# Attention's numerators in 64 array rows and 256 columns a call, with the units loaded by quarters of the partitions

## The chip, the cores and the metric

One core of a Trainium2 chip runs the kernel. The metric is the device time of one launch in microseconds (us). The engines are named as in the profile: PE (TensorE matmuls), PEld (TensorE weight loads), DVE (VectorE), ACT (ScalarE), POOL (GpSimd) and SP (SyncE, which here only issues DMAs). Each engine works through its own list of instructions in order.

## The reference

A block of a transformer: 2048 tokens, width 1024, 32 heads of 32, a hidden layer of 3584. Attention is linear, with a learned feature map of two softmaxes:

```python
def _A_ref(x, wqkv, w_phi, wo):
    q, k, v = ...                        # x @ wqkv, by heads
    pq = einsum("bhsd,hdf->bhsf", q, w_phi)
    pk = einsum("bhsd,hdf->bhsf", k, w_phi)
    phi_q = concatenate([softmax(pq), softmax(-pq)], axis=-1)
    phi_k = concatenate([softmax(pk), softmax(-pk)], axis=-1)
    kv = einsum("bhsf,bhsd->bhfd", phi_k, v)
    z  = einsum("bhsf->bhf", phi_k)
    num = einsum("bhqf,bhfd->bhqd", phi_q, kv)
    den = einsum("bhqf,bhf->bhq", phi_q, z)[..., None] + 1e-6
    o = num / den
    return o (heads side by side) @ wo
h  = x + _A_ref(layernorm(x), wqkv, w_phi, wo)
h2 = h + relu(layernorm(h) @ w1) @ w2
```

The map gives 64 features for a head: 32 of the positive sign and 32 of the negative. In the text, "sign" is this half of the features.

## The kernel before, in words

The program is one long list of items of eight steps. A step is three matmuls of 128x512 (`mm3`, L182 to L184), because each fp32 operand is split into a high and a low part. Beside the steps stands a table, `at[n, k]`: the work that is to be written into the program before step k of item n. `when(8 * n + k, f)` and `do(n, k, f)` fill it. So the order of everything beside the large matmuls, on every engine, follows from numbers in this table; at run time an engine waits when the head of its own list is not ready.

The items run in this order: keys and values of the first 1024 tokens (`kv`, 32 items), queries of them (`q`, 16), keys and values of the second 1024 tokens, their queries, the output projection (`wo`), then the two layers of the feed-forward part (`up`, `down`). The `wo` items begin at item `wo_first`.

**Feature map of q.** `q_first` (DVE) takes maximum and minimum and writes both signs' arguments into a tile; `q_second` (ACT) exponentiates and stores the 512 KB tile to DRAM (`ed`); `q_third` (DVE) sums over the 32 features and inverts (`smq`, the softmaxes' inverse sums, kept in SBUF).

**Sums over k.** `kv_third` (PE, L464) accumulates kv for four heads at a time; at the end `kv_turn` transposes it with TensorE to `kvL` and `z_sum` adds the keys' features over the partitions (`zb`).

**Attention units.** The rest is cut into 32 units u, each of four token tiles (one of four groups b) and four of the 32 heads. For each unit run, in this order:

- `at_load` (SP, L543): one DMA of 512 KB from `ed`; `at_sums` (POOL, L575): two products with `zb`, 128x512 each; `at_reduce` (DVE, L581): their sums over 32 features;
- `at_den` (POOL, L591 and L595): times the inverse sums, and the two signs added, which lie side by side in the free dimension; `at_inverse` (DVE, L598);
- `at_scale` (POOL, L608 and L613): inverse sum times inverse denominator, and the 128x1024 product of the unit with it; `at_turn` (DVE, L619): transposition in blocks of 32x32.

After an odd unit, `at_num` (PE, L633) multiplies the pair by `kvL`: 64 calls in tiles of 32 rows and 32 columns of the array, 128 tokens a call, which the profile shows as 128 records. Each PSUM bank has a row group's results; four banks are used, two of the pool `tp` (two banks in all, which transposes use too) and two of `ac`. ACT copies the four banks to `oT` (L640), and `at_low` (DVE, L651) takes the rest of the split, four times.

I number the pairs k = 0 to 15; units 2k and 2k+1 are E and O below. Units 0 to 5 have sums and denominators done early. From u = 12 the steps of an even unit are, relative to its start, 7 for the load, 14 sums, 18 reduce, 20 denominator, 22 inverse, 24 scale, 28 turn; `at_num` comes at step 38 and `at_low` at step 40. So a pair's `at_low` is written while the next pair's denominators are under way. The first units of `wo` overlap with the last groups of the attention.

**The second layer norm's first half** also runs in the `wo` stage: `ln_pair` has nine stages for each i = 0..3 (load, statistics, power, normalize, three turns of four TensorE transposes each, one with sums, one more with sums), and `ln_store` stores the results. `NEAR` gives their steps.

The weights' splitting (L125 on ACT, L129 on POOL or DVE) goes on all the time.

Of the kernel before, what the change touches and what calls it, by code (L numbers as in the profile page):

```python
# [140 lines left out]
def kernel(  # L141
# [55 lines left out]
    ed = [dram.tile([P, 8, 4, 256], F32, name=f"ed{b}") for b in range(4)]  # L197
# [257 lines left out]
    def kv_third(key):  # L455
# [12 lines left out]
        for g in range(2):  # L468
            ps = kv_ps[s][g][:, 0:64]
            if hf == 0:  # L470
                v.tensor_copy(kvacc[s][:, g, :], ps)
            else:
                kd_of[s, g] = kd = kp.tile([P, 2, 4, 32], F32, name="kd", bufs=2)
                for sd in range(2):
                    part = slice(32 * sd, 32 * (sd + 1))
                    v.tensor_add(kd[:, sd, :, :], ps[:, None, part].to_broadcast([P, 4, 32]),
                                 kvacc[s][:, g, None, part].to_broadcast([P, 4, 32]))

    def kv_turn(s):
        pt = tp_bank()  # L480
        for g in range(2):
            for sd in range(2):
                pe.transpose(pt[:, (2 * sd + g) * P:(2 * sd + g + 1) * P],
                             kd_of[s, g][:, sd].rearrange("p c f -> p (c f)"), ident)
        v.tensor_copy(kvL[:, 4 * s:4 * s + 4, :], pt.rearrange("p (g n) -> p g n", g=4))

    def z_sum(s):


        pz = tp_bank()  # L490
        pe.matmul(pz, ones, zacc[s], start=True, stop=True)
        act.activation(zb[:, s, :].rearrange("p (r c x) -> p c r x", r=2, c=4),
                       pz.rearrange("p (c r x) -> p c r x", r=2, c=4), AF.Identity, bias=eps)
# [17 lines left out]
    def q_first(s, t, ps):  # L511

        pq = ps.rearrange("p (h f) -> p h f", f=32)
        m = pqp.tile([P, 2, 16], F32, name="qmx", bufs=2)
        v.tensor_reduce(out=m[:, 0, :], in_=pq, op=ALU.max, axis=AX.X)
        v.tensor_reduce(out=m[:, 1, :], in_=pq, op=ALU.min, axis=AX.X)
        e = pqp.tile([P, 16, 2, 32], F32, name="qe", bufs=2)
        v.tensor_sub(e[:, :, 0, :], pq, m[:, 0, :, None].to_broadcast([P, 16, 32]))
        v.tensor_sub(e[:, :, 1, :], m[:, 1, :, None].to_broadcast([P, 16, 32]), pq)
        e_of[s, t] = e  # L520

    def q_second(s, t):
        act.activation(e_of[s, t], e_of[s, t], AF.Exp)
        b, i = place_of[t]
        act.dma_start(ed[b][:, 4 * s:4 * s + 4, i, :], e_of[s, t].rearrange("p (a c) s f -> p a (c s f)", a=4))

    def q_third(s, t):
        b, i = place_of[t]
        sm = smq[:, 4 * b + i, 32 * s:32 * (s + 1)]
        v.tensor_reduce(out=sm, in_=e_of.pop((s, t)).rearrange("p h s f -> p (h s) f"), op=ALU.add, axis=AX.X)  # L530
        v.reciprocal(sm, sm)

# [6 lines left out]
    def at_load(u):  # L539

        e = lnp.tile([P, D], F32, name="xin") if u in (4, 5, 10, 11) else ap_.tile([P, D], F32, name="qe", bufs=4)
        e_q[u] = e = e.rearrange("p (h s f) -> p h s f", s=2, f=DH)
        sp.dma_start(e.rearrange("p (i c) s f -> p i (c s f)", i=4), ed[u // 8][:, u % 8])  # L543

# [4 lines left out]
    def early_load(u):  # L549
        e_q[u] = e = xlp.tile([P, D], F32, name="xl").rearrange("p (h s f) -> p h s f", s=2, f=DH)  # L550
        sp.dma_start(e.rearrange("p (i c) s f -> p i (c s f)", i=4), ed[u // 8][:, u % 8])

    def early_sums(u):
        b, q, r = UNITS[u]
        e = e_q[u].rearrange("p (i h) s f -> p i (h s f)", i=4)
        pool.tensor_tensor(out=e, in0=e, in1=zb[:, q, None, 256 * r:256 * (r + 1)].to_broadcast([P, 4, 256]),
                           op=ALU.mult)

    def early_reduce(u):
        tz_of[u] = tz = xlp.tile([P, 32], F32, name="xtz", bufs=2)  # L560
        v.tensor_reduce(out=tz, in_=e_q.pop(u).rearrange("p h s f -> p (h s) f"), op=ALU.add, axis=AX.X)

    def early_scale(u):
        den = den_of.pop(u)
        sm = sm_half(u).rearrange("p i (h s) -> p i h s", s=2)
        pool.tensor_tensor(out=sm, in0=sm, op=ALU.mult,
                           in1=den.rearrange("p (i h) -> p i h", i=4)[:, :, :, None].to_broadcast([P, 4, 4, 2]))

    def at_sums(u):

        b, q, r = UNITS[u]
        for j in range(2):
            third = hp is not None and (2 * u + j) % 3 == 2
            ez_of[u, j] = ez = (hp if third else ap_).tile([P, 2, 256], F32, name="ez", bufs=1 if third else 2)
            pool.tensor_tensor(out=ez, in0=e_q[u].rearrange("p (i h) s f -> p i (h s f)", i=4)[:, 2 * j:2 * j + 2, :],  # L575
                               in1=zb[:, q, None, 256 * r:256 * (r + 1)].to_broadcast([P, 2, 256]), op=ALU.mult)

    def at_reduce(u):
        tz_of[u] = tz = ap_.tile([P, 32], F32, name="qtz", bufs=2)
        for j in range(2):  # L580
            v.tensor_reduce(out=tz[:, 16 * j:16 * (j + 1)], in_=ez_of.pop((u, j)).rearrange("p i (h f) -> p (i h) f", f=DH),  # L581
                            op=ALU.add, axis=AX.X)

    def sm_half(u):
        b, q, r = UNITS[u]
        return smq[:, 4 * b:4 * b + 4, 16 * q + 8 * r:16 * q + 8 * r + 8]

    def at_den(u):

        tz = tz_of.pop(u)  # L590
        pool.tensor_tensor(out=tz.rearrange("p (i h) -> p i h", i=4), in0=tz.rearrange("p (i h) -> p i h", i=4),  # L591
                           in1=sm_half(u), op=ALU.mult)
        tz2 = tz.rearrange("p (h s) -> p h s", s=2)
        den_of[u] = den = (ap_ or xlp).tile([P, 16], F32, name="qden", bufs=2)
        pool.tensor_tensor(out=den, in0=tz2[:, :, 0], in1=tz2[:, :, 1], op=ALU.add)  # L595
# [4 lines left out]
    def at_scale(u):  # L600
        if u < EARLY:
            e = e_q.pop(u).rearrange("p (i c) s f -> p i (c s) f", i=4)
            pool.tensor_tensor(out=e, in0=e, in1=sm_half(u)[:, :, :, None].to_broadcast([P, 4, 8, 32]), op=ALU.mult)
# [706 lines left out]
```

## Time and profile before

| | |
|---|---|
| median of 3 runs | 1883.05 us (1880.56, 1883.05, 1883.9) |
| the profiled execution: its time, its span | 1883.67 us, 1881.9 us |
| PE busy | 1871.4 us, 99% |
| DVE, ACT, POOL busy | 1070.6, 739.0, 973.1 us |
| clock granted to TensorE | 0.999 |
| attention's numerators on PE (L633) | from 552.0 us to 759.9 us |

A busy share counts an engine over the whole span, over stages with different limits. The attention's part of the trace, 550 to 760 us, is where the change works, so stage views of that part are read below.

### The profile page before, as it was taken

How to read it: one execution, taken by the hardware profiler on the slowest of the kernel's cores; microseconds unless marked ns; L12 is line 12 of the kernel's file. 1: busy time of each engine (PE TensorE's matmuls, PEld its weight loads, DVE VectorE, ACT ScalarE, POOL GpSimd, SP SyncE). 2: the span in 40 equal slices, each digit the busy share in tenths (PEclk: the TensorE clock that was granted, in tenths of full speed). 3: DMA queues.
4: the chain of work that ended last, by engine and by line, in shares of the span. 5: the costliest groups of instructions: out<-in, count | busy, mean ns of one | idle time of the engine just before them, and what ended most of it. 6: DMA issues, size and time to landing. Idle time of an engine off the chain costs nothing.

```text
span 1881.9 us, 31799 instructions
## 1 busy us (share of the span) xinstructions
PE 1871.4 (99%) x11608; PEld 1535.3 (82%) x11608; DVE 1070.6 (57%) x1695; ACT 739.0 (39%) x1271; POOL 973.1 (52%) x959
## 2 busy tenths in 40 slices
PE   9999999999999999999999999999999999999999
PEld 7877788888787888878888888888888888888887
DVE  7788688677689777555554563444433333343333
ACT  5322245222233122255455554444444444444442
POOL 4887744888946988333233222222344444444443
PEclk9999999999999999999999999999999999999999
DMA  6888788656565666887888985666677677767775
GB/s 225 290 293 289 227 296 258 199 190 200 185 217 177 203 226 221 259 258 217 258 254 263 320 273 176 192 191 215 210 238 215 204 228 238 238 213 219 216 216 178
DMA packets 303277, 432.17 MB, mean 230 GB/s; under 512 B 24208, under 2 KB 165520, under 8 KB 303120
## 3 DMA queue, kind: packets, MB, share of 16 engines
q1 hardware_dynamic: 286224, 413.36, 70.0%
q10 hardware_dynamic: 16896, 16.78, 2.7%
q8 instruction: 91, 1.49, 0.3%
q14 instruction: 66, 0.54, 0.1%
HBM read 292.68 MB, written 137.36 MB: 229 GB/s over the span
## 4 chain that ended last, share of the span: by engine, by line
PE 95%; DMA 2%; POOL 1%; DVE 1%; issue 0%; ACT 0%; SPq 0%; DVEq 0%; ACTq 0%; POOLq 0%
PE mm L182 25%; PE mm L183 24%; PE mm L184 24%; PE ac L183 4%; PE ac L182 4%; PE ac L184 4%; PE tp L183 2%; PE tp L184 2%; PE tp L182 2%; PE tp L245 1%; PE ac L464 1%; PE tp L633 1%; DMA hT<-hs 1%; DMA hs<-xin 1%; PE ac L633 1%; POOL w L129 0%
## 5 line engine op out<-in xcount | busy, mean ns | idle before, releaser
L129 POOL TENSOR_TENSOR w<-raw,w 128x512 fp32r<-128x512 f32 x353 | 469.2, 1331 | 719.8 <-ACT w L125 674.8
L125 ACT ACTIVATE w<-raw 128x512 fp32r<-128x512 f32 x686 | 409.0, 626 | 508.0 <-PE mm L184 235.0
L129 DVE TENSOR_TENSOR w<-raw,w 128x512 fp32r<-128x512 f32 x333 | 271.4, 816 | 519.5 <-ACT w L125 514.1
L182 PE MATMUL mm<-w,xT 128*128 128x512 f32 x768 | 305.3, 398 | 0.0
L183 PE MATMUL mm<-w,xT 128*128 128x512 f32 x768 | 299.8, 390 | 0.6 <-POOL w L400 0.4
L184 PE MATMUL mm<-w,xT 128*128 128x512 f32 x768 | 299.3, 390 | 0.0
L183 PE MATMUL mm<-hT,w 128*128 128x512 f32 x672 | 262.1, 390 | 2.8 <-DVE hT L829 2.8
L182 PE MATMUL mm<-hT,w 128*128 128x512 f32 x672 | 262.2, 390 | 0.0
L184 PE MATMUL mm<-hT,w 128*128 128x512 f32 x672 | 262.0, 390 | 0.0
L362 POOL TENSOR_TENSOR b<-b 128x256 f32<-128x256 f32 x176 | 143.5, 816 | 55.1 <-DMA b<-in_w_dram 36.9
L182 PEld LDWEIGHTS mm<-w,xT 128*128 128x128 f32 x768 | 144.2, 188 | 33.9 <-issue 2.9
L184 PEld LDWEIGHTS mm<-w,xT 128*128 128x128 f32 x768 | 144.2, 188 | 30.7
L183 PEld LDWEIGHTS mm<-w,xT 128*128 128x128 f32 x768 | 144.3, 188 | 29.9 <-POOL w L129 1.0
L182 PE MATMUL mm<-w 128*128 128x512 f32 x392 | 152.5, 389 | 0.0
L183 PE MATMUL mm<-w 128*128 128x512 f32 x392 | 152.5, 389 | 0.0
L184 PE MATMUL mm<-w 128*128 128x512 f32 x392 | 152.5, 389 | 0.0
L183 PEld LDWEIGHTS mm<-hT,w 128*128 128x128 f32 x672 | 126.6, 188 | 29.6 <-DVE hT L829 3.3
L184 PEld LDWEIGHTS mm<-hT,w 128*128 128x128 f32 x672 | 126.6, 188 | 26.4
L182 PEld LDWEIGHTS mm<-hT,w 128*128 128x128 f32 x672 | 126.4, 188 | 26.3
L182 PEld LDWEIGHTS mm<-w 128*128 128x128 f32 x392 | 73.6, 188 | 15.3
L183 PEld LDWEIGHTS mm<-w 128*128 128x128 f32 x392 | 73.6, 188 | 15.3
L184 PEld LDWEIGHTS mm<-w 128*128 128x128 f32 x392 | 73.6, 188 | 15.2
(184 smaller groups left out, 3147.9 us busy)
## 6 DMA issues: line engine op xcount, KB each, us to landing
raw<-t SPq DMA_DIRECT2D x224, 256.0 KB, 3.9
raw<-ad SPq DMA_DIRECT2D x196, 256.0 KB, 3.0
raw<-in_w_dram SPq DMA_DIRECT2D x168, 256.0 KB, 3.1
ad<-c SPq DMA_DIRECT2D x112, 256.0 KB, 3.6
b<-in_w_dram SPq DMA_DIRECT2D x44, 512.0 KB, 6.0
t<-b SPq DMA_DIRECT2D x44, 512.0 KB, 4.8
ad<-s SPq DMA_DIRECT2D x84, 256.0 KB, 3.9
ed<-qe ACTq DMA_DIRECT2D x32, 512.0 KB, 4.4
```

The source lines that it names most:

```text
L125: nc.scalar.activation(w[:, 0, :], raw[1], AF.Copy)
L129: eng.tensor_tensor(out=w[:, 1, :], in0=raw[1], in1=w[:, 0, :].bitcast(F32), op=ALU.subtract)
L182: pe.matmul(ps, a_hi, b_hi, start=first, stop=False, skip_group_check=more)
L183: pe.matmul(ps, a_hi, b_lo, start=False, stop=False, skip_group_check=more)
L184: pe.matmul(ps, a_lo, b_hi, start=False, stop=last, skip_group_check=more)
L245: pe.transpose(pt[:, k, :], xn[:, (4 * j + k) * P:(4 * j + k + 1) * P], ident)
L362: pool.tensor_tensor(out=tsum[*u, *out], in0=tsum[*u, *a], in1=tsum[*u, *b], op=ALU.subtract)
L464: pe.matmul(kv_ps[s][g][32 * i:32 * (i + 1), 0:64], vt[:, 32 * h:32 * (h + 1)], phi[:, 64 * h:64 * (h + 1)], start=first, stop=last)
L633: pe.matmul(banks[g][32 * c:32 * (c + 1), j * P:(j + 1) * P], kvL[rows, 4 * q + 2 * sd + h // 4, 32 * (h % 4):32 * (h % 4 + 1)], phT_of[u ...
```

## The change

Four pieces belong together.

1. **Numerators.** `at_num` has 16 calls: 64 rows (both signs of 32 features) and 256 columns. It fills two banks of `ac`, and none of `tp`. ACT then copies two banks of 512 columns, and `at_low` has two instructions. `kvL` therefore holds both signs along the rows, `kv_turn` does two TensorE transposes for four heads where it had four, and `kd` is made with one addition.

2. **Layout.** For 64 rows both signs of the same tokens must lie in neighbouring blocks of 32 partitions once a unit has been turned. So `q_first` writes the tile sign by sign in groups of four heads, and `by_quarter` reads a unit in four DMAs of 32 partitions each: a quarter has one sign and one pair of token tiles. Each of the 32 units has four loads of 128 KB where it had one of 512 KB. The inverse sums `smq` are needed in the same layout: `sm_store` writes them to DRAM and `sm_load` reads them back in four DMAs (`smx`), once for each of the four groups.

3. **Denominators.** The two signs of a token now lie in different partitions. `at_den` keeps its first product; the new `at_cross` copies four 32x32 blocks on ACT to the other sign's partitions, and the new `at_add` (POOL) adds. The inverse (DVE) and the products have 32 columns, where the inverse had 16. `z_sum` writes `zb` in four ACT instructions of 32 partitions where it had one.

4. **Steps.** The lists of steps get the two new stages, and `NEAR` becomes one list for all i, by which the turns of a pair are written as eight transposes twice. Some fill in the SBUF pools is smaller.

```diff
-    ed = [dram.tile([P, 8, 4, 256], F32, name=f"ed{b}") for b in range(4)]
+    ed = [dram.tile([8, 4, P, 256], F32, name=f"ed{b}") for b in range(4)]
+    smd = [dram.tile([4, P, 64], F32, name=f"smd{b}") for b in range(4)]
...
+    def by_quarter(dst, src):
+        for a in range(4):
+            sp.dma_start(dst[32 * a:32 * (a + 1)],
+                         src[2 * (a // 2):2 * (a // 2) + 2].rearrange("i (n t) (s x) -> s t (i n) x", t=32, s=2)[a % 2])
...
     def at_den(u):
-        tz = tz_of.pop(u)
-        pool.tensor_tensor(out=tz.rearrange("p (i h) -> p i h", i=4), in0=tz.rearrange("p (i h) -> p i h", i=4),
-                           in1=sm_half(u), op=ALU.mult)
-        tz2 = tz.rearrange("p (h s) -> p h s", s=2)
-        den_of[u] = den = (ap_ or xlp).tile([P, 16], F32, name="qden", bufs=2)
-        pool.tensor_tensor(out=den, in0=tz2[:, :, 0], in1=tz2[:, :, 1], op=ALU.add)
+        tz = tz_of[u].rearrange("p (n c) -> p n c", n=8)
+        pool.tensor_tensor(out=tz, in0=tz, in1=sm_half(u), op=ALU.mult)
+    def at_cross(u):
+        den_of[u] = den = (ap_ or xlp).tile([P, 32], F32, name="qden", bufs=2)
+        for a in range(4):
+            act.activation(den[32 * (a ^ 1):32 * (a ^ 1) + 32], tz_of[u][32 * a:32 * (a + 1)], AF.Copy)
+    def at_add(u):
+        pool.tensor_tensor(out=den_of[u], in0=tz_of.pop(u), in1=den_of[u], op=ALU.add)
...
     def at_num(u):
-        acc_of[u] = banks = tp_bank(), tp_bank(), ac_bank(), ac_bank()
-        for sd in range(2):
-            for j in range(2):
-                for g in range(4):
-                    rows = slice(32 * g, 32 * (g + 1))
-                    for c in range(4):
-                        pe.matmul(banks[g][32 * c:32 * (c + 1), j * P:(j + 1) * P], ...)
+        acc_of[u] = banks = ac_bank(), ac_bank()
+        for j in range(2):
+            for g in range(2):
+                rows = slice(64 * g, 64 * (g + 1))
+                for c in range(4):
+                    pe.matmul(banks[g][32 * c:32 * (c + 1), 256 * j:256 * (j + 1)], ...)
...
-        stages = (-8, 6, 10, 13, 16, 19, 25) if u < 12 else (7, 14, 18, 20, 22, 24, 28) if u % 2 == 0 else \
-            (-1, 9, 13, 15, 17, 19, 23)
+        stages = (-8, 6, 10, 13, 15, 17, 18, 20, 26) if u < 12 else (7, 14, 18, 20, 21, 23, 24, 25, 29) if u % 2 == 0 else \
+            (-1, 9, 13, 15, 16, 18, 19, 20, 24)
...
-    NEAR = {1: (0, 9, 12, 17, 29, 30, 31, 32, 34, 37), 2: (4, 14, 17, 21, 25, 26, 27, 28, 30, 36)}
+    NEAR = 0, 9, 12, 17, 24, 24, 27, 27, 30, 36
```

The pair k = 12 (units 24 and 25) shows how the lists of POOL, DVE and ACT change. In these rows a name's number tells one tile from another. First POOL before, from the first denominator to the first product of the next pair: `qtz_8311` and `qden_8324` belong to E, `qtz_8329` and `qden_8413` to O.

```order
L591 TENSOR_TENSOR qtz_8311<-qtz_8311,smq_2995 128x32
L595 TENSOR_TENSOR qden_8324<-qtz_8311 128x16
L591 TENSOR_TENSOR qtz_8329<-qtz_8329,smq_2995 128x32
L595 TENSOR_TENSOR qden_8413<-qtz_8329 128x16
L608 TENSOR_TENSOR qsd_8427<-smq_2995,qden_8324 128x32
L613 TENSOR_TENSOR qe_8226<-qe_8226,qsd_8427 128x1024
L608 TENSOR_TENSOR qsd_8441<-smq_2995,qden_8413 128x32
L613 TENSOR_TENSOR qe_8228<-qe_8228,qsd_8441 128x1024
L575 TENSOR_TENSOR ez_8460<-qe_8415,zb_2993 128x512
```

Both denominators are whole before E is scaled. POOL in the changed kernel, at the same place, where `qden_7946` is E's and `qden_8000` O's:

```order
L602 TENSOR_TENSOR qtz_7930<-qtz_7930,smx_3000 128x32
L611 TENSOR_TENSOR qden_7946<-qtz_7930,qden_7946 128x32
L602 TENSOR_TENSOR qtz_7951<-qtz_7951,smx_3000 128x32
L624 TENSOR_TENSOR qsd_8020<-smx_3000,qden_7946 128x32
L627 TENSOR_TENSOR qe_7834<-qe_7834,qsd_8020 128x1024
L611 TENSOR_TENSOR qden_8000<-qtz_7951,qden_8000 128x32
L624 TENSOR_TENSOR qsd_8050<-smx_3000,qden_8000 128x32
L627 TENSOR_TENSOR qe_7839<-qe_7839,qsd_8050 128x1024
L586 TENSOR_TENSOR ez_8060<-qe_7983,zb_2997 128x512
```

The addition of O (L611 of `qden_8000`) has moved behind the scaling of E, and each addition now reads a tile that ACT has written in between.

DVE before, from E's last sums, with the previous pair's `at_low` (L651, `oT_7834`):

```order
L581 TENSOR_REDUCE qtz_8311<-ez_8287 128x16
L581 TENSOR_REDUCE qtz_8329<-ez_8301 128x16
L581 TENSOR_REDUCE qtz_8329<-ez_8303 128x16
L598 RECIPROCAL qden_8324<-qden_8324 128x16
L651 TENSOR_TENSOR oT_7834<-tp_8335,oT_7834 128x8x32
L651 TENSOR_TENSOR oT_7834<-tp_8336,oT_7834 128x8x32
L651 TENSOR_TENSOR oT_7834<-ac_8337,oT_7834 128x8x32
L651 TENSOR_TENSOR oT_7834<-ac_8338,oT_7834 128x8x32
L598 RECIPROCAL qden_8413<-qden_8413 128x16
L688 TENSOR_TENSOR xh_8230<-mm_8294,xh_8230 128x512
L619 STREAM_TRANSPOSE qe_8226<-qe_8226 128x1024
```

E's inverse (`qden_8324`) stands ahead of the previous pair's `at_low`. DVE in the changed kernel (`at_low` is L663, the inverse L614):

```order
L592 TENSOR_REDUCE qtz_7930<-ez_7906 128x16
L592 TENSOR_REDUCE qtz_7951<-ez_7920 128x16
L592 TENSOR_REDUCE qtz_7951<-ez_7922 128x16
L663 TENSOR_TENSOR oT_7526<-ac_7957,oT_7526 128x2x256
L663 TENSOR_TENSOR oT_7526<-ac_7958,oT_7526 128x2x256
L614 RECIPROCAL qden_7946<-qden_7946 128x32
L700 TENSOR_TENSOR xh_7844<-mm_7912,xh_7844 128x512
L614 RECIPROCAL qden_8000<-qden_8000 128x32
L740 TENSOR_TENSOR s12_8038<-s12_8038,xin_7771 128x512
L741 TENSOR_TENSOR xin_7771<-xin_7769,s12_8038 128x512
L633 STREAM_TRANSPOSE qe_7834<-qe_7834 128x1024
```

E's inverse (`qden_7946`) stands behind the previous pair's two `at_low`, and O's behind one more addition of the output projection.

ACT before, around the copies of the previous pair's banks (L640):

```order
L238 ACTIVATE xin_8110<-xin_8110,sc_8271 128x1024
L238 ACTIVATE xin_8112<-xin_8112,sc_8275 128x1024
L640 ACTIVATE oT_7834<-tp_8335 128x8x32
L640 ACTIVATE oT_7834<-tp_8336 128x8x32
L640 ACTIVATE oT_7834<-ac_8337 128x8x32
L640 ACTIVATE oT_7834<-ac_8338 128x8x32
L247 ACTIVATE xin_8110<-tp_8451 128x512
```

ACT in the changed kernel, with the new copies of the denominators (L608) and the banks' copies (L653):

```order
L239 ACTIVATE xin_7771<-xin_7771,sc_7893 128x1024
L608 ACTIVATE qden_7946<-qtz_7930 32x32 x4
L653 ACTIVATE oT_7526<-ac_7957 128x2x256
L653 ACTIVATE oT_7526<-ac_7958 128x2x256
L608 ACTIVATE qden_8000<-qtz_7951 32x32 x4
L248 ACTIVATE xin_7769<-tp_8005 128x512
```

The four copies of E's products stand ahead of the previous pair's bank copies, those of O behind them.

135 lines of the change are left out of this document (70 added, 65 removed).

## The prediction

> **What bounds the kernel now.** I read the page first: its chain, then the stage views where the change works, then single rows. Of the chain, shares by engine; then two stretches of the attention, where the columns are length, and busy time of PE, PEld, DVE, ACT and POOL with the number of instructions, then clock, DMA share and GB/s:
>
> ```profile
> PE 95%; DMA 2%; POOL 1%; DVE 1%; issue 0%; ACT 0%; SPq 0%; DVEq 0%; ACTq 0%; POOLq 0%
> ```
> ```profile
> 560.00:624.00 64.00, 63.54 (x804) 51.29 (x810) 61.15 (x99) 19.76 (x37) 46.92 (x48) 1.00 0.59 196
> 620.00:760.00 140.00, 140.00 (x1952) 113.81 (x1950) 103.67 (x179) 26.84 (x59) 122.76 (x154) 1.00 0.68 220
> ```
>
> PE sets the end: it is without gaps in both stretches, at full clock. So what PE has less to do comes off the time, if the feeding engines keep up. Here they are close: from 560 to 624 DVE is busy for 61.15 of 64 us, and from 620 to 760 POOL for 122.76 of 140. DVE has the turns, POOL the sums and scalings, and `at_num` needs both. The change shortens PE's part and lengthens POOL's and DVE's waits, so I price both.
>
> **PE's part.** What the numerators take out of the matmul stream, by the starts around one `at_num`:
>
> ```profile
> 551.47 0.39 PE L183 MATMUL mm<-w,xT 128*128 128x512 f32 x1
> 551.70 0.39 PE L184 MATMUL mm<-w,xT 128*128 128x512 f32 x1
> 552.01 0.34 PE L633 MATMUL tp<-qe,kvL 32*32 32x128 f32 x8
> ...
> 554.18 0.39 PE L183 MATMUL mm<-w,xT 128*128 128x512 f32 x1
> ```
>
> Starts in the plain stream are 0.23 us apart (551.47, 551.70). From 551.70 to 554.18 are 2.48 us, of which two large matmuls (L184 and the L182 in between) take 0.46: 2.02 us for 128 records. Sixteen pairs: 32.3 us. Each of the 16 places of 32x32 in the array gets 8 records of 128 columns. After, a position of 64x32 gets 4 of 256 columns, 32 records over 8 places: the same 1024 columns each, so the streaming as such is not shorter, only the number of instructions. The nearest row is the fold of the weights, 64 records of 256 columns in 32x32 tiles, again 1024 columns a place:
>
> ```profile
> 99.27 0.39 PE L184 MATMUL mm<-w,xT 128*128 128x512 f32 x1
> 99.58 0.44 PE L290 MATMUL tp<-wt,wphi 32*32 32x256 f32 x8
> ...
> 101.35 0.40 PE L183 MATMUL mm<-w,xT 128*128 128x512 f32 x1
> ```
>
> From 99.27 to 101.35 are 2.08 us, less 0.46: 1.62. So 64 records fewer saved 0.40 (0.0062 each), and 32 fewer still would save 0.20: 1.42 us is my estimate for the new `at_num`. The bounds are 1.62 and 1.0, the latter from the accumulation of kv, 48 records in whole columns of 128 rows:
>
> ```profile
> 97.17 0.88 PE L464 MATMUL ac<-kphi,vt 128*32 128x64 f32 x48
> 670.96 0.60 PE L245 MATMUL tp<-ident,xin 128*128 128x128 f32 x4
> ```
>
> The gain is 0.60 a pair, 9.6 in all (6.4 to 16.3). The second row is of four TensorE transposes, 0.60: two fewer in each of four `kv_turn` are worth 0.3 at most each; I take 0.9 together. Writing the layer norm's transposes in eights changes no number of transposes on PE: nothing, and what could be late, the bank copies, lies beside several steps. With all else hidden, PE's list gives 9.6 + 0.9 = 10.5 us less.
>
> The Trainium skill, page "TensorE: Matmul & The Clock Gate", Part 3 (packing small matmuls), says that a weight load overlaps a running matmul only where the row group differs. The calls of one `at_num` now come four by four in the same 64 rows; I price this as a rival. The row of L464, all in one row group, does not bear it out.
>
> **POOL's cycle.** Pair 12 (units 24 and 25) shows a cycle without foreign work. POOL, from the first product with `zb` to that of the next pair:
>
> ```profile
> 700.87 5.02 POOL L575 TENSOR_TENSOR ez<-qe,zb 128x512 f32<-128x512 f32 x4
> 705.86 0.24 POOL L591 TENSOR_TENSOR qtz<-qtz,smq 128x32 f32<-128x32 f32 x1
> 706.18 0.21 POOL L595 TENSOR_TENSOR qden<-qtz 128x16 f32<-128x16 f32 x1
> 706.69 0.26 POOL L591 TENSOR_TENSOR qtz<-qtz,smq 128x32 f32<-128x32 f32 x1 [0.30 <-DVE qtz L581]
> 707.03 0.21 POOL L595 TENSOR_TENSOR qden<-qtz 128x16 f32<-128x16 f32 x1
> 707.20 0.24 POOL L608 TENSOR_TENSOR qsd<-smq,qden 128x32 f32<-128x32 f32 x1
> 707.52 1.92 POOL L613 TENSOR_TENSOR qe<-qe,qsd 128x1024 f32<-128x1024 f32 x1
> 709.40 0.24 POOL L608 TENSOR_TENSOR qsd<-smq,qden 128x32 f32<-128x32 f32 x1
> 709.72 1.92 POOL L613 TENSOR_TENSOR qe<-qe,qsd 128x1024 f32<-128x1024 f32 x1
> 711.59 2.53 POOL L575 TENSOR_TENSOR ez<-qe,zb 128x512 f32<-128x512 f32 x2
> ```
>
> That is 10.72 us, hardly a wait in it; E's scaling starts 6.65 after the first product. On DVE and ACT beside it:
>
> ```profile
> 706.53 0.24 DVE L598 RECIPROCAL qden<-qden 128x16 f32<-128x16 f32 x1
> 706.69 0.69 DVE L651 TENSOR_TENSOR oT<-tp,oT 128x256 fp32r<-128x256 f32 x2
> 707.29 0.75 DVE L651 TENSOR_TENSOR oT<-ac,oT 128x256 fp32r<-128x256 f32 x2
> ```
> ```profile
> 704.56 0.66 ACT L640 ACTIVATE oT<-tp 128x256 fp32r<-128x256 f32 x2 [2.36 <-PE tp L633]
> ```
> ```profile
> L762 ACT ACTIVATE scx<-tp 128x64 f32<-128x64 f32 x1 | 0.2, 218 | 0.0
> ```
>
> The third view, with mean ns in the column after the busy time, has the smallest ACT copy, 218 ns; nothing in the trace is a copy of 32x32 to other partitions, and I take 0.22 (between 0.1 and 0.4).
>
> By the order, after the change E's inverse waits for this: E's product done at 5.23 (706.10 less 700.87); four copies of 0.22, 6.11; then ACT copies the previous pair's first bank (two of 256 columns take 0.66), 6.77; the two `at_low` on DVE, which stand ahead of the inverse (706.69 to 708.04, 1.35), 8.12; inverse 0.3 (0.24 with half the columns), 8.42; inverse sum times it, 0.32 to the scaling's start: 8.74 where it was 6.65. Then the scaling takes 1.87 (709.72 to 711.59), 10.61; only now O's addition 0.21, O's inverse 0.3, the small product 0.32, 11.44; O's scaling 1.87: 13.31. Rows of one engine overlap by 0.05 to 0.1 (706.69 + 0.69 is past 707.29); I take off 0.3 for these: **13.0 us a pair**, 2.3 more than before. Who waits for the waiting POOL: the turn of the same unit, and behind it `at_num` on PE; queued behind it are the next pair's products.
>
> PE gave a pair 12.94 us where no layer norm turn falls in (717.58 to 730.52 below), and after the change 12.3. So POOL's loop, hidden before with 2.2 us to spare, is 0.7 longer than PE's.
>
> ```profile
> 620.18 2.54 POOL L575 TENSOR_TENSOR ez<-qe,zb 128x512 f32<-128x512 f32 x2 [0.42 <-DMA qe<-ed]
> ```
> ```profile
> 717.58 0.34 PE L633 MATMUL tp<-qe,kvL 32*32 32x128 f32 x8
> ...
> 730.52 0.34 PE L633 MATMUL tp<-qe,kvL 32*32 32x128 f32 x8
> ...
> 758.22 0.34 PE L633 MATMUL tp<-qe,kvL 32*32 32x128 f32 x8
> ```
>
> From pair 6's first product (620.18) to the last `at_num` (758.22) before: 138.0 us. After: ten loops, 130.0; the last turn 1.3; and POOL's other work, the weight splits and layer norm powers. The stretch of 140 us holds some 10.4 pairs, 111 us of POOL, so 11.5 of its 122.76 is other work, of which I count 9, the rest falling into waits. Together 140.3, 2.3 more than before.
>
> **Pair 6's start** is set by the load. Rows of SP, of 128 KB loads in the same shape (32 partitions, rows of 512 B), and of the DMA issues (KB, us to landing):
>
> ```profile
> 616.23 0.90 SPq L543 DMA_DIRECT2D qe<-ed  x2
> ```
> ```profile
> L774 SPq DMA_DIRECT2D xin<-hd x32: 539/604/652, 855.4 to 1001.5; - x32
> ```
> ```profile
> qe<-ed SPq DMA_DIRECT2D x28, 512.0 KB, 5.4
> ...
> xin<-hd SPq DMA_DIRECT2D x32, 128.0 KB, 5.5
> ```
>
> Issue takes SP 0.60 for a quarter, where one of two whole loads took 0.45; landing takes as long as for a whole one. Four instead of one: 2.4 − 0.45, about 2.0 us later. Against that, PE arrives earlier, by 0.9 and at most five `at_num` of 0.60; but DVE, full from 560 to 624, has no less to do (four `at_low` in 1.35 before; two of twice the width after), so I let 0.7 of it through. Pair 6 starts 1.3 later. So the last `at_num` comes 1.3 + 2.3 = 3.6 later and is 0.6 shorter: **+3.0 us**. The loads' other cost, the early units' longer denominators and the 16 transfers of the sums' quarters, lies behind the kv items' slack; its price without that cover is the same 2 us once.
>
> The Trainium skill, page "DMA: Bandwidth & Descriptors", section "Rules for kernel authors", says of two transfers to disjoint partition halves that they serialize on the same engines, and to use one of 128 partitions. This trace has 5.5 us for a quarter and 5.4 for the whole, so a quarter costs no less; by the rule in full, four landings one behind the other would be an estimated 22 us a unit, for which I see no row.
>
> The profiled execution took 1883.67 us, 0.6 above the median of 1883.05. The sums are differences, so I set them on the median: 1886.0.
>
> **The rivals.**
>
> *POOL's loop stays hidden* (faster). If the new waits overlap more than my sum has it (copies at 0.1, `at_low` done before E's product), the loop is under 12.3 and PE's list decides: 1883.05 − 10.5 = 1872.5. For it: PE alone is 95% of the chain, and POOL's cycle had slack. Against: the order puts `at_low` ahead of the inverse, and O's addition behind E's scaling.
>
> *The loads come late* (slower). Two units before a pair's products:
>
> ```profile
> 692.01 1.97 SPq L543 DMA_DIRECT2D qe<-ed  x2
> ```
>
> These two loads are of pair 12, issued 8.9 us ahead of its first product at 700.87. After, eight quarters of 0.60 and 5.5 to land are 10.3 for O's last, needed at 8.9 + 2.5 = 11.4: 1.1 to spare. If a landing lengthens by more than that, with the DMA engines 0.68 busy, POOL waits in each pair; 2 us each over ten pairs give 20, about 1904.
>
> *The call itself is not shorter* (slower; the change doesn't do what it says). If each weight load waited for the matmul before it in its rows, `at_num` would show at least 32 loads of 0.10 us:
>
> ```profile
> L633 PEld LDWEIGHTS ac<-qe,kvL x896: 101/104/106, 552.1 to 759.7; 32*32 32x32 f32 x180
> ```
>
> That is 3.3 us instead of 2.02; 16 × 1.3 = 20 where PE decides, about 1902.
>
> **How the numbers follow.** The forecast, POOL's loop as the bound, has 0.50; POOL hidden 0.25; loads late 0.15; the call not shorter 0.05; 0.05 for others. A measurement of this kernel tells some 0.2% from no change, 3.8 us: 1879.3 to 1886.8. The forecast's own range is 1880 to 1893: loops of 12.7 to 13.4 give −3 and +4, the start of pair 6 −2 to +3. About 0.22 of its 0.50 falls below 1886.8 and above 1879.3, 0.05 below, 0.23 above. Faster is then 0.05 + 0.25 + 0.02 = 0.32, the same 0.22, slower 0.23 + 0.15 + 0.05 + 0.03 = 0.46. The range takes in POOL hidden with a somewhat better `at_num` (1870) and late loads up to 1902.
>
> **What would show it.** Right: `at_num` at 1.4 us; POOL idle before L624 waiting for DVE L614, some 2 us a pair, and about 13 us from pair to pair; PE idle before or in its weight loads of `at_num`, waiting for DVE's turn. Wrong: no PE idle from 550 to 760, and the last `at_num` ten us earlier; or POOL's L586 waiting for DMA in most pairs; or an `at_num` over 2 us.

## The result, and the profile after

The changed kernel takes 1904.4 us (median of four runs, 1901.26 to 1904.85) against 1882.55 (four runs, 1880.56 to 1883.9): slower by a ratio of 1.0112, 95% interval 1.01 to 1.0125. I had forecast 1886, with a range of 1870 to 1902. The page's chain by engine, and the two stretches of before (same columns):

```profile
PE 85%; POOL 5%; DVE 3%; DMA 3%; issue 2%; SPq 1%; ACT 1%; POOLq 0%; DVEq 0%; ACTq 0%
```
```profile
560.00:624.00 64.00, 60.83 (x379) 46.21 (x377) 58.00 (x88) 25.03 (x53) 41.88 (x44) 0.97 0.66 177
620.00:760.00 140.00, 117.69 (x748) 88.69 (x747) 92.98 (x138) 37.52 (x106) 107.96 (x131) 0.98 0.77 200
```

PE, without a gap before, is idle for 22.3 of the 140 us from 620 to 760. Nobody else is full: POOL fell from 122.76 to 107.96 busy us. So the time goes into waits from engine to engine. PE's own part did become shorter. PE's timeline around the first `at_num`, and the start of the last:

```profile
551.03 0.39 PE L184 MATMUL mm<-w,xT 128*128 128x512 f32 x1
551.35 1.09 PE L646 MATMUL ac<-qe,kvL 64*32 64x256 f32 x32
...
552.71 0.40 PE L183 MATMUL mm<-w,xT 128*128 128x512 f32 x1
...
779.75 1.22 PE L646 MATMUL ac<-qe,kvL 64*32 64x256 f32 x32
```

From 551.03 to 552.71 are 1.68 us, less 0.46 for two large matmuls: 1.22 us, where I had estimated 1.42. The last `at_num` starts at 779.75, 21.5 us after the 758.22 of before. That is the whole loss: it lies between 550 and 780. What in it is new can be read off POOL's rows. From pair 6's first product to the end of the last scaling, each row counted to the start of the next and the waits taken apart, they add up to this (us, rounded):

| | pairs' own instructions | other work | waits | together |
|---|---|---|---|---|
| before | 107.4 | 19.1 | 9.9 | 136.4 |
| changed | 107.2 | 19.3 | 28.5 | 155.1 |

POOL has the same work in both, and only its waits have grown. Now one cycle of POOL, pair 7, with no foreign work in it:

```profile
640.75 5.00 POOL L586 TENSOR_TENSOR ez<-qe,zb 128x512 f32<-128x512 f32 x4
645.71 0.25 POOL L602 TENSOR_TENSOR qtz<-qtz,smx 128x32 f32<-128x32 f32 x1
647.09 0.25 POOL L611 TENSOR_TENSOR qden<-qtz,qden 128x32 f32<-128x32 f32 x1 [1.12 <-ACT qden L608]
647.30 0.25 POOL L602 TENSOR_TENSOR qtz<-qtz,smx 128x32 f32<-128x32 f32 x1
649.23 0.25 POOL L624 TENSOR_TENSOR qsd<-smx,qden 128x32 f32<-128x32 f32 x1 [1.68 <-PE mm L184]
649.56 1.92 POOL L627 TENSOR_TENSOR qe<-qe,qsd 128x1024 f32<-128x1024 f32 x1
651.44 0.25 POOL L611 TENSOR_TENSOR qden<-qtz,qden 128x32 f32<-128x32 f32 x1
652.16 0.25 POOL L624 TENSOR_TENSOR qsd<-smx,qden 128x32 f32<-128x32 f32 x1 [0.47 <-DVE qden L614]
652.49 1.92 POOL L627 TENSOR_TENSOR qe<-qe,qsd 128x1024 f32<-128x1024 f32 x1
654.36 5.00 POOL L586 TENSOR_TENSOR ez<-qe,zb 128x512 f32<-128x512 f32 x4
```

The cycle is 13.61 us, where it was 10.72, and three waits are new: 1.12 for the copies on ACT, 1.68 for E's inverse, 0.47 for O's. The one put down to PE is a wait for DVE's inverse, as the other engines in the same stretch show:

```profile
646.00 0.95 ACT L608 ACTIVATE qden<-qtz 32x32 f32<-32x32 f32 x4 [10.58 <-POOL qtz L602]
646.97 1.09 ACT L653 ACTIVATE oT<-ac 128x512 fp32r<-128x512 f32 x2
```
```profile
647.60 1.29 DVE L663 TENSOR_TENSOR oT<-ac,oT 128x512 fp32r<-128x512 f32 x2 [1.13 <-ACT oT L653]
648.81 0.34 DVE L614 RECIPROCAL qden<-qden 128x32 f32<-128x32 f32 x1
```

This is the chain that the prediction worked out from the order: copies on ACT, the previous pair's bank copies, `at_low`, the inverse. PE pays for it in front of `at_num`, where from 600 to 780 it waits some 6 us for DVE's turns, and, more than I had thought of, in front of the layer norm's transposes:

```profile
718.44 0.39 PE L184 MATMUL mm<-w,oT 128*128 128x512 f32 x1
723.77 1.12 PE L246 MATMUL tp<-ident,xin 128*128 128x128 f32 x4 [4.94 <-ACT xin L248]
```

There are three such stalls, with 3.4, 5.3 and 5.1 us from start to start. The second, shown here, is a wait for a PSUM bank: the copies that free it (L248) stand in ACT's list behind the new copies of the denominators, which wait for POOL's product:

```profile
720.07 0.94 ACT L608 ACTIVATE qden<-qtz 32x32 f32<-32x32 f32 x4 [3.92 <-POOL qtz L602]
...
723.12 1.09 ACT L248 ACTIVATE xin<-tp 128x512 f32<-128x512 f32 x2
```

The other two are waits for the normalization on ACT (L239). The stalls raised the question that the experiments begin with: is the slow part the denominators' cycle, the transposes in eights, or the loads?

### The profile page after: what moved, and what is told of

It reads as the page before. It is cut to its first block, busy times and chain, and to the rows that moved or that the text cites. A ratio compares the mean times of both kernels' runs of the same rounds, so it can differ in the third digit from the quotient of the medians.

```text
span 1902.3 us, 29047 instructions
## 1 busy us (share of the span) xinstructions
PE 1866.5 (98%) x10064; PEld 1519.7 (80%) x10064; DVE 1071.3 (56%) x1655; ACT 770.2 (40%) x1379; POOL 972.7 (51%) x959
## 4 chain that ended last, share of the span: by engine, by line
PE 85%; POOL 5%; DVE 3%; DMA 3%; issue 2%; SPq 1%; ACT 1%; POOLq 0%; DVEq 0%; ACTq 0%
PE mm L182 22%; PE mm L183 22%; PE mm L184 21%; PE ac L183 4%; PE ac L182 4%; PE ac L184 4%; PE tp L183 2%; PE tp L182 2%; PE tp L184 2%; POOL ez L586 2%; DMA hT<-hs 1%; PE ac L465 1%; POOL qe L627 1%; PE tp L246 1%; POOL w L129 1%
## 5 line engine op out<-in xcount | busy, mean ns | idle before, releaser
L184 PEld LDWEIGHTS mm<-w 128*128 128x128 f32 x392 | 73.6, 188 | 15.3
L182 PEld LDWEIGHTS mm<-w 128*128 128x128 f32 x392 | 73.6, 188 | 15.3
L183 PEld LDWEIGHTS mm<-w 128*128 128x128 f32 x392 | 73.6, 188 | 15.3
```

The source lines that it names most:

```text
L182: pe.matmul(ps, a_hi, b_hi, start=first, stop=False, skip_group_check=more)
L183: pe.matmul(ps, a_hi, b_lo, start=False, stop=False, skip_group_check=more)
L184: pe.matmul(ps, a_lo, b_hi, start=False, stop=last, skip_group_check=more)
```

## The experiments

Ratios are to runs of the kernel before on the same chip; the time of the changed kernel to compare with is 1904.4.

**The layer norm's steps of before.**

```diff
-    NEAR = 0, 9, 12, 17, 24, 24, 27, 27, 30, 36
+    NEAR = {1: (0, 9, 12, 17, 29, 30, 31, 32, 34, 37), 2: (4, 14, 17, 21, 25, 26, 27, 28, 30, 36)}
...
+        ln2 = NEAR.get(i, (0, 9, 12, 17, 24, 25, 26, 27, 29, 36))
```

> The changed kernel, with the layer norm's steps of before (transposes in fours, i = 1 and 2 at their own steps). Theory 'the cycle' (POOL's cycle of a pair, 13.61 us in the changed kernel, sets the pace; PE's stalls at the layer norm's transposes are mostly time that it would wait for at_num anyway): 1898 to 1902, 3 to 6 us off, for the POOL waits of 1.6 and 3.8 us that lie behind DVE work stalled by PE. Rival 'the eights' (the stalls of 3.4, 5.3 and 5.1 us at the transposes, and the slow steps behind them, are lost time): 1888 to 1892, 13 to 16 off. Rival 'the loads': no change, 1904.

Measured: 1907.57 (1904.97 to 1907.89), ratio 1.013 (1.0113 to 1.0147). Nothing is won, so the eights are not the cause of the changed kernel's loss. It also missed the small gain that I expected from the cycle. The undisturbed cycle is 13.6 as in the changed kernel, and PE still waits 6.5 us at the transposes, for the normalization: their input is late.

**E's inverse ahead of `at_low`.**

```diff
-        ... (7, 14, 18, 20, 21, 23, 24, 25, 29) if u % 2 == 0 ...
+        ... (7, 14, 18, 20, 20, 22, 23, 25, 29) if u % 2 == 0 ...
```

> The changed kernel, with four steps of the even units earlier by one, so that E's inverse stands ahead of the previous pair's two at_low on DVE. The cycle: the wait of 1.68 us before E's small product falls to about 0.4, a cycle of 12.3, ten cycles: 1890 to 1894. The eights, the loads: 1903 to 1905.

Measured: 1902.88 (1902.24 to 1904.74), ratio 1.0111 (1.0096 to 1.0126). That is no gain, the time that I had given the other two theories. Yet the edit did what it was to do. POOL's cycle, first row to last, and then what PE waited for from 600 to 780 (us, times, longest):

```profile
653.51 5.05 POOL L586 TENSOR_TENSOR ez<-qe,zb 128x512 f32<-128x512 f32 x4
...
660.61 0.26 POOL L624 TENSOR_TENSOR qsd<-smx,qden 128x32 f32<-128x32 f32 x1 [0.26 <-DVE qden L614]
...
665.75 1.30 POOL L586 TENSOR_TENSOR ez<-qe,zb 128x512 f32<-128x512 f32 x1
```
```profile
PE tp L246 <- ACT xin L239: 7.2, 2, 4.4
PE tp L246 <- ACT xin L248: 5.0, 1, 5.0
```

The cycle went from 13.61 to 12.24, but the pairs with layer norm work on POOL still took 15.3 to 18.7 us (14.7 to 17.5 in the changed kernel), and the stalls at the transposes stayed. POOL's rows show why so little came of it. In four of these pairs E's small product had waited only 0.26 us in the changed kernel already, because layer norm work stood in the gap, so there the edit had nothing to save. What it saved elsewhere went in good part into POOL's waits for DVE's sums: 2.25 us in pair 6, where there had been none, and 4.92 in pair 14, where it had been 3.77. The last `at_num` started 2.0 us earlier, at 777.77.

**No copies and no additions.**

```diff
     def at_cross(u):
-        den_of[u] = den = ... ; for a in range(4): act.activation(...)
+        den_of[u] = tz_of.pop(u)
     def at_add(u):
-        pool.tensor_tensor(out=den_of[u], ...)
+        return
```

> The changed kernel without the copies on ACT and without the additions: each sign is divided by its own half of the denominator. The cycle: the waits of 1.12 us before the addition and most of the 1.68 go, and O's addition and inverse lie beside E's scaling: a cycle of 11.5 to 12, PE's own pace; what is left over PE's list is the layer norm's stalls: 1872 to 1883. The eights: 1895 or more, since the transposes are where they were. The loads: 1900.

Measured: 1887.53 (1884.57 to 1891.24), ratio 1.0027 (1.0018 to 1.0037). So 17 of the 22 us hang on the exchange between the signs. The cycle, 11.70, is what I gave for this case, but the time is above its range: POOL still waits 1.57 and 5.11 us for DVE's sums in two pairs with layer norm work, which I hadn't counted.

**Whole loads.**

```diff
-        by_quarter(e, ed[u // 8][u % 8])
+        sp.dma_start(e.rearrange("p (i s) x -> p i (s x)", i=4), ed[u // 8][u % 8].rearrange("i p x -> p i x"))
```

> The changed kernel with one DMA of 512 KB and 128 partitions a unit in place of four quarters (the elements then stand at other places of the tile; same sizes of work). The cycle: only the two waits of POOL for loads, 1.2 and 4.3 us, can go: 1899 to 1903. The loads: 1885 to 1890. The eights: 1904.

Measured: 1903.36 (1902.61 to 1907.13), ratio 1.0116 (1.0101 to 1.0131): within 2 us of the changed kernel. The quarters alone are not the cause, although the last `at_num` starts 3.0 us earlier (776.70); the time shows 1 us of that. Pair 6 starts at 623.75 with whole loads and at 623.79 with quarters, so its delay isn't theirs either.

**The addition on DVE, E's inverse ahead of `at_low`.**

```diff
     def at_add(u):
-        pool.tensor_tensor(out=den_of[u], in0=tz_of.pop(u), in1=den_of[u], op=ALU.add)
+        v.tensor_add(den_of[u], tz_of.pop(u), den_of[u])
...
+        ... (7, 14, 18, 20, 21, 22, 22, 25, 29) ... (-1, 9, 13, 15, 16, 17, 17, 20, 24)
```

> The changed kernel with the denominators' addition on DVE directly ahead of the inverse (no hop to POOL in between, O's addition no longer behind E's scaling), and E's inverse ahead of at_low. The copies stay on ACT. Theory 'POOL's lag' (whatever POOL feeds comes late because its cycle is longer than PE's 12.1 us): a cycle of 11.9 us, 1885 to 1892. Rival 'ACT tied' (the new copies stand in ACT's list ahead of bank copies and of the layer norm's normalization, and hold these until POOL has got to the next denominators): 1896 to 1902.

Measured: 1896.6 (1894.55 to 1899.25), ratio 1.0078 (1.0062 to 1.0093), with a cycle of 12.07. The cycle came out near the 11.9 of the first theory, the time in the range of the second. That the copies on ACT hold ACT's other work would fit this, and PE still waits 3.0 us for a bank that L248 frees (5 in the changed kernel); the next runs take the copies off ACT.

**Copies and addition on DVE.**

```diff
-            act.activation(den[32 * (a ^ 1):32 * (a ^ 1) + 32], tz_of[u][32 * a:32 * (a + 1)], AF.Copy)
+            v.tensor_copy(den[32 * (a ^ 1):32 * (a ^ 1) + 32], tz_of[u][32 * a:32 * (a + 1)])
...
+        ... (-8, 6, 10, 13, 15, 15, 15, 20, 26) if u < 12 else (7, 14, 18, 20, 22, 22, 22, 25, 29) ... (-1, 9, 13, 15, 15, 15, 15, 20, 24)
```

> As the run with the addition on DVE, and the four copies on DVE too; ACT has no part in the denominators. POOL's lag: from the product to the small product 0.6 + 0.25 + 0.35 us on DVE, E's scaling some 7.1 us after the cycle's start, O's directly behind it, a cycle of 11.2: 1872 to 1884. ACT tied: the same range, and over 8 us below the run that leaves the copies on ACT; by POOL's lag alone the two differ by 7 us at most.

> As the run with copies and addition on DVE, and the layer norm's steps of before. Either theory: within 4 us of that run. If the eights still cost something once POOL is in time: 5 to 12 below it.

Measured: 1912.39 (1910.66 to 1913.24), and 1907.24 (1905.32 to 1909.31) with the layer norm's steps of before. Both were misses, by 28 us for the first. The steps of before took 5.2 us off here, clear of the runs' spread and in the range that I had given for eights that cost something of their own. DVE's timeline shows two groups of the same four copies, and POOL's row tells them apart:

```profile
640.95 0.77 DVE L608 COPY qden<-qtz 32x32 f32<-32x32 f32 x4 [0.77 <-POOL qtz L602]
...
642.37 2.36 DVE L608 COPY qden<-qtz 32x32 f32<-32x32 f32 x4
```
```profile
642.74 1.94 POOL L627 TENSOR_TENSOR qe<-qe,qsd 128x1024 f32<-128x1024 f32 x1
```

Alone the copies take 0.77. Where POOL's product starts while they are under way they end at 644.73, when the product ends (644.68). And units 6 to 11, which have their denominators where DVE is full, now came later: `at_num` of pair 4 at 618.5, where the changed kernel has 610.6.

**The numerators alone.** The kernel before with the new `at_num`, its two bank copies and two `at_low`, and nothing else of the change.

> The kernel before with only at_num in 16 calls of 64 rows and 256 columns in two banks, two bank copies and two at_low; loads, layout and denominators as before, so the numerators mix the two signs in a wrong way. By PE's list: 1.23 us for 2.04, 16 times, 13.0 us off: 1868 to 1872 if the feeding engines keep up; 1876 to 1880 if half of it is eaten, because POOL and DVE then set the pace from 560 to 624.

Measured: 1874.79 (1874.35 to 1875.54), ratio 0.9961 (0.9946 to 0.9976). So the part of the change that shortens PE's list is worth about 7 us here, with POOL's cycle as before (643.76 to 654.51, 10.75 us):

```profile
643.76 5.04 POOL L575 TENSOR_TENSOR ez<-qe,zb 128x512 f32<-128x512 f32 x4
...
654.51 1.30 POOL L575 TENSOR_TENSOR ez<-qe,zb 128x512 f32<-128x512 f32 x1
```

**Additions on DVE without copies, from unit 12,** where units before 12 stay as in the changed kernel.

```diff
+                v.tensor_tensor(out=den[32 * a:32 * a + 32], in0=tz_of[u][32 * a:32 * (a + 1)],
+                                in1=tz_of[u][32 * (a ^ 1):32 * (a ^ 1) + 32], op=ALU.add)
```

> The changed kernel; from unit 12 the denominators are four DVE additions of 32x32 that read the other sign's partitions directly (no copies, no ACT, no POOL addition), both inverses ahead of at_low; units before 12 as in the changed kernel. What the run with copies on DVE showed: a copy of 32x32 on DVE beside POOL's 128x1024 scaling, four in 2.36 us, four in 0.73 without. If only copies are held so (an addition was 0.19 beside it): a cycle of 11.2 to 11.8, 1880 to 1888. If additions with 32 partitions are held likewise: a cycle over 13 again, 1898 to 1905.

> As the run with additions on DVE, and one DMA of 512 KB a unit (other places of the elements). If the 8 issues of 0.6 us on SP hold the layer norm's loads and the statistics (the wait of DVE for them, 4.2 us in the run with only the addition on DVE) once the cycle is shorter: 4 to 8 below that run. If not: within 2.

> As the run with additions on DVE, and the layer norm's steps of before (fours). If the eights cost something of their own once POOL is in time: 4 to 10 below that run; if the stalls at the transposes only show POOL's lag: within 3 of it.

Measured: 1901.13 (1898.26 to 1902.9); with whole loads 1899.22 (1896.82 to 1899.55); with the layer norm's steps of before 1897.02 (1895.32 to 1901.24). The additions were held like the copies, as DVE's rows and POOL's product beside the second show:

```profile
644.32 0.77 DVE L611 TENSOR_TENSOR qden<-qtz 32x32 f32<-32x32 f32 x4
...
645.51 2.54 DVE L611 TENSOR_TENSOR qden<-qtz 32x32 f32<-32x32 f32 x4
```
```profile
645.89 1.92 POOL L633 TENSOR_TENSOR qe<-qe,qsd 128x1024 f32<-128x1024 f32 x1
```

The cycle was 12.2, under the 13 that I had set for this case, with the time in that case's range all the same. The steps' effect (4.1 us) and the loads' (1.9) overlap with the spread of the runs; neither is shown.

**A longer cycle in the kernel before.** The counter-test: POOL repeats a small product, and all else is as before.

```diff
+        for _ in range(5 if u % 2 == 0 else 4) if u >= 12 else ():
+            pool.tensor_tensor(out=sd..., in0=sm_half(u)..., in1=den..., op=ALU.mult)
```

> The kernel before; from unit 12 POOL repeats the small product (qsd, 0.32 us from start to start) five times in an even and four times in an odd unit, ahead of the scaling: 2.9 us more in a pair's cycle, 10.72 becomes 13.6; loads, layout, numerators and layer norm as before. If POOL's cycle alone sets the time: pair 6 starts at 620.2 as before, and the 156 us from there to the last at_num that the changed kernel took bring it to 776, 18 us late: 1898 to 1903. If the changed kernel's loads, ACT copies or eights had half a part: 1888 to 1893.

Measured: 1906.94 (1906.19 to 1908.04), ratio 1.0131 (1.0114 to 1.0148). The cycle (first and last row below) is 13.64, and the last `at_num` starts at 779.22, half a us from the changed kernel's (inside it, it waits another 2.9 us for the turn of its second unit):

```profile
651.27 5.02 POOL L575 TENSOR_TENSOR ez<-qe,zb 128x512 f32<-128x512 f32 x4
...
664.91 1.29 POOL L575 TENSOR_TENSOR ez<-qe,zb 128x512 f32<-128x512 f32 x1
```
```profile
779.22 0.34 PE L638 MATMUL tp<-qe,kvL 32*32 32x128 f32 x8 [1.04 <-issue]
```

A cycle of this length is enough for a loss of this size, without quarters, without copies on ACT, without eights. It isn't a copy of the changed kernel, though: here POOL is busy in the added time and all its other work comes on top, while in the changed kernel it waits and part of that work fits into the waits.

**One-input instructions on DVE, from unit 12.** POOL writes its product into every second column; DVE fetches the other sign's half by reductions over one element and sums the pair by a reduction.

```diff
+                v.tensor_reduce(out=two_of[u][32 * (a ^ 1):32 * (a ^ 1) + 32, :, 1],
+                                in_=two_of[u][32 * a:32 * (a + 1), :, 0:1], op=ALU.add, axis=AX.X)
...
+            v.tensor_reduce(out=den_of[u], in_=two_of.pop(u), op=ALU.add, axis=AX.X)
```

> The changed kernel; from unit 12 POOL's product goes into pairs, DVE fetches the other sign's half with four reductions over one element and sums with a reduction, so that each of these instructions has one SBUF input; no ACT copies, no POOL addition, both inverses ahead of at_low. If such instructions are not held by POOL's 128x1024 product: 4 x 0.2 + 0.2 + 0.35 us, a cycle of 11.2, 1878 to 1886. If they are held too: as with additions, 1898 to 1903.

Measured: 1894.41 (1891.91 to 1895.57), ratio 1.0062 (1.0047 to 1.0077), the fastest version of the whole change that I found, and still slower than before. DVE's second group and POOL's product:

```profile
645.63 0.75 DVE L616 TENSOR_REDUCE qtwo<-qtwo 32x32 f32<-32x32 f32 x4
```
```profile
646.01 1.92 POOL L640 TENSOR_TENSOR qe<-qe,qsd 128x1024 f32<-128x1024 f32 x1
```

The reductions are not held: 0.75 beside the product. The cycle is 11.64 to 11.68, not 11.2; POOL waits 0.59 and 1.17 us for DVE in it, some 0.45 more than I had summed. What is left shows on SP and DVE:

```profile
726.91 4.11 SPq L541 DMA_DIRECT2D qe<-ed  x8
...
731.99 4.41 SPq L216 DMA_DIRECT2D xin<-hd  x2
```
```profile
737.28 1.29 DVE L222 BATCH_NORM_STATS2 st<-xin 128x6 f32<-128x512 f32 x2 [3.23 <-DMA xin<-hd]
```

The eight quarters of a pair occupy SP for 4.1 us ahead of the layer norm's loads; DVE waits for these, POOL behind DVE, and PE stalls at the transposes.

**Loads again, now with the short cycle.**

```diff
-            sp.dma_start(dst[32 * a:32 * (a + 1)],
+            queue.dma_start(dst[32 * a:32 * (a + 1)],
...
-        by_quarter(e, ed[u // 8][u % 8])
+        by_quarter(e, ed[u // 8][u % 8], act if u >= 12 else sp)
```

> As the run with one-input reductions on DVE, and one DMA of 512 KB a unit (other places of the elements). If the quarters on SP's queue are the second part: 1884 to 1888, 6 to 10 below the 1894.4 of that run. If what is left is only POOL's cycle (11.64 against 10.72, with 19 us of its other work): 1892 to 1895.

> As the run with one-input reductions on DVE; from unit 12 the four DMAs of a unit are issued by ACT in place of SP, so that they don't stand ahead of or behind the layer norm's DMAs. If the quarters on SP's queue are the second part: 1880 to 1888, pair 6 up to 3 us earlier as well. If only the cycle counts: 1892 to 1895.

> As the run with the quarters on ACT's queue, and the layer norm's steps of before. With POOL and the loads in time, the transposes find their input at either place: within 3 us of that run. If the steps of before (i = 1 five steps later) still help: 4 to 8 below it, and below the kernel before.

Measured: 1888.9 (1886.31 to 1889.22), ratio 1.0034 (1.0021 to 1.0047), with whole loads: 5.5 below the run with one-input instructions, a little less than I had given. So here the quarters do cost. With whole loads DVE no longer waits for the layer norm's loads (3.23 and 1.23 us with quarters), and POOL's list from pair 6 on takes 136.7 us, as long as before; at the last `at_num`, 3.1 us behind the kernel before (761.36 against 758.22), only the later start of pair 6 (623.68) is left.

Issued by ACT the quarters made it worse, 1908.93 (1907.86 to 1914.39), and 1916.86 (1913.8 to 1921.57) with the layer norm's steps of before besides. Both were misses. ACT's DMA row:

```profile
659.21 10.85 ACTq L541 DMA_DIRECT2D qe<-ed  x8
```

Eight issues took 10.85 us, and ACT's bank copies and normalizations stood behind them.

## Why the prediction was wrong

**PE's part: right in kind, small in size.** `at_num` is 1.22 us (1.42 forecast, bounds 1.0 and 1.62), and the kernel before gains from it alone, about 7 us of a possible 16 × 0.8 = 13. So the call is shorter, and the rival of weight loads that wait falls.

**POOL's cycle: the right mechanism.** POOL waits before L624 for DVE's inverse, 1.68 and 0.47 us a pair, as the prediction said it would. The cycle was mis-sized by little: E's scaling starts 8.81 us after the first product (8.74 by the full durations), and O's addition, inverse and small product take 1.05 (0.83), which makes 13.61 where full durations gave 13.31. I had taken 0.3 off for overlap that wasn't there. Ten cycles: 6.1 us.

**What failed is the sum of the stretch.** It had ten cycles, 9 for POOL's other work and 1.3 for the last turn: 140.3 from pair 6's first product to the last `at_num`, where the trace has 779.75 − 623.79 = 156.0. Apart from the cycles:

- The other work was misread: 11.5 us, of which 2.5 would fall into waits. POOL's rows of before already have 19.1, and those of the changed kernel 19.3. In four pairs (9, 10, 14 and 15) it stood in the waits for the exchange, so that the 1.12 and 1.68 before E's addition and small product fell to nothing and 0.26; that takes 10.2 off. So 9.2 came on top, and the 9 was right by luck.
- Put at nothing, without a reason, was what else makes a pair with layer norm work longer than the undisturbed one: 5.4 us of waits for DVE's sums, 3.8 in which POOL's own instructions of the pairs ran longer than ten undisturbed cycles have it, and 0.7 in one wait for O's inverse. Together some 10 us, the largest of the errors. Pair 9 shows the first kind and the small wait before L624; DVE's rows beside it, then the same place in the kernel before:

```profile
667.97 3.76 POOL L586 TENSOR_TENSOR ez<-qe,zb 128x512 f32<-128x512 f32 x3
673.32 1.29 POOL L586 TENSOR_TENSOR ez<-qe,zb 128x512 f32<-128x512 f32 x1 [1.59 <-DVE qtz L592]
...
678.12 0.25 POOL L624 TENSOR_TENSOR qsd<-smx,qden 128x32 f32<-128x32 f32 x1 [0.26 <-DVE qden L614]
...
683.24 5.48 POOL L586 TENSOR_TENSOR ez<-qe,zb 128x512 f32<-128x512 f32 x4
```
```profile
671.22 1.23 DVE L222 BATCH_NORM_STATS2 st<-xin 128x6 f32<-128x512 f32 x2
...
672.61 1.82 DVE L592 TENSOR_REDUCE qtz<-ez 128x16 f32<-128x512 f32 x3
```
```profile
664.28 1.29 POOL L575 TENSOR_TENSOR ez<-qe,zb 128x512 f32<-128x512 f32 x1 [5.05 <-DVE qtz L581]
```

  The layer norm's statistics stand ahead of the sums in DVE's list, and POOL's fourth product waits behind them. The pair takes 15.27 us: 1.59 of the 1.66 over an undisturbed one is this wait. The kernel before has two such waits, 5.05 and 3.14, so the term could have been read there.
- Pair 6 starts at 623.79, 3.6 later than before and not 1.3. The quarters didn't make it late (the run with whole loads). POOL was through with pair 5, whose denominators have the same chain, 2.8 later than before, and then waited 1.23 for the load, whose issue came 1.9 later (618.16 against 616.23).

The cycles' 6.1, the other 10 and the start's 2.3, less 0.4 for the last turn, make 18.0. The last `at_num` was forecast 3.6 late and came 21.5 late, 17.9 more.

**The rivals.** "POOL's loop stays hidden" falls by the trace (a cycle of 13.61, with PE waiting) and by the counter-test. "The loads come late", priced at 1904, has the right time for the wrong reason: whole loads took 1 us off while the cycle was long. They count, with 5.5 us, only when it is short. That the layer norm would be where PE pays was in none of my cases. The eights cost the changed kernel nothing that the runs show, but the steps do matter in other orders, with either sign: those of before gave +3.2, −5.2, −4.1 and +7.9 us in four runs, the last two with spreads that overlap. Why the sign changes is not settled.

**POOL's list in the other runs,** counted as in the table above (the counter-test's repeated products are in its own instructions):

| | pair 6 starts | own | other work | waits | together |
|---|---|---|---|---|---|
| no copies and no additions | 621.8 | 102.6 | 19.4 | 17.5 | 139.6 |
| counter-test | 620.9 | 137.3 | 19.2 | 3.9 | 160.4 |
| one-input instructions, whole loads | 623.7 | 102.6 | 19.5 | 14.6 | 136.7 |

So the other work is the same everywhere; what differs is the waits and, in the counter-test, the added instructions. With quarters and a cycle of 11.6 to 12.2, POOL's longest wait is for DVE's sums in pair 14, 4.9 to 6.2 us; in front of it DVE waits for the layer norm's loads, 3.6 us in all with E's inverse ahead, 4.2 with the addition on DVE, 4.5 with one-input instructions. With whole loads DVE has no such wait.

**What stays open.** The rows name these waits one by one; how many us of the end each is worth was measured for the exchange (17) and, with the short cycle, for the quarters (5.5), not for the others. How much ACT's held copies cost by themselves is not measured either: every run without them changed the cycle too.

## What to carry to other kernels

A gain on the engine that bounds the kernel counts only as far as its feeders' cycles stay under the new pace: add up a feeder's whole list, with its waits, for the stretch, and not its busy share (POOL was busy for 108 us of 140 and set the time). A hand-over between engines inside a cycle cost its full durations here (13.61 us measured, 13.31 summed). Other work of the waiting engine fills such a gap only where it is ready at that moment (half of 19 us here), and it brings waits of its own. When a layout change needs data from other partitions, price that exchange first: here it cost 17 us, more than twice what the larger calls brought.

## What the hardware showed that I had not expected

**DVE held by POOL.** Four DVE instructions of 32x32 took 0.77 us alone and 2.36 (copies) or 2.54 (additions of two SBUF inputs) when POOL's 128x1024 product ran beside them; four reductions of the same size took 0.75 either way. The Trainium skill, page "SBUF — State Buffer", section "Who interferes with whom", says that a copy in a two-port mode and an instruction with two SBUF inputs contend with POOL for a shared port, and that reductions on trn2 don't. These rows agree: copies and two-input additions were held, reductions weren't. In which mode the copies ran no row shows.

**Slow matmuls after a stall.** After the stall of 5.3 us the large matmuls started 0.43 us apart instead of 0.23, here two of nine in a row, and were back to 0.23 from 729.65 on. The granted clock, the third column from the end in the stretch view below, was 0.52 meanwhile:

```profile
726.39 0.63 PE L184 MATMUL mm<-w,oT 128*128 128x512 f32 x1
726.82 0.63 PE L182 MATMUL mm<-w,oT 128*128 128x512 f32 x1
...
729.65 0.39 PE L183 MATMUL mm<-w,oT 128*128 128x512 f32 x1
729.88 0.40 PE L184 MATMUL mm<-w,oT 128*128 128x512 f32 x1
```
```profile
725.30:729.60 4.30, 4.30 (x13) 3.43 (x12) 3.54 (x4) 0.88 (x2) 3.76 (x5) 0.52 0.21 64
```

The stall of 5.1 us was followed by a clock of 0.54 (760 to 762) and the same slow steps until 763.3; after the one of 3.4 us the clock stayed at 1.00. So this stall of PE cost some 2 us more than its length, which no term of mine had.
